# Linear attention and a rational feed-forward layer on one core: first unit in two halves of the head pairs, all of w_in cast by its DMA, early loads ordered by holds, a new list of steps

## Chip, cores and metric

The kernel runs on one core of one Trainium2 chip. The metric is the device time of the core in microseconds (us); smaller is better.

## The reference, cut

```python
# attention: batch 4, heads 8, sequence 768, head size 48
f = 1.0 / (1.0 + np.exp(-f_logit))
for t in range(S):
    state = f[:, :, t, :, None] * state + np.einsum('bhd,bhe->bhde', k[:, :, t], v[:, :, t])
    y[:, :, t] = np.einsum('bhd,bhde->bhe', q[:, :, t], state)
x = y.transpose(0, 2, 1, 3).reshape(B * S, H * D)        # 3072 x 384
# feed-forward: w_in 384 x 2048, w_out 2048 x 384
h = x @ w_in
P = a[0] + a[1] * h + a[2] * h**2 + a[3] * h**3
Q = 1.0 + np.abs(b[0]) * np.abs(h) + np.abs(b[1]) * h**2
out = (P / (Q + 1e-06)) @ w_out
```

## The kernel before

The work is cut into 12 units (3 chunks of 256 positions for each of 4 batch entries). One unit first goes through attention on all 8 heads: exp and log of f (`efl`), a running sum over positions by a triangular matmul (`cs`), exponentials of it (`A0`, `A1`), products with q and k (`mq`, `mk`), transposes (`T`) and their copy out of PSUM (`Te`), scores (`sc0`, `sc1`), masks (`m0`, `m1`), state (`sv`, `st`, `su`), `y`, and `xT` (`xe`). Then it goes through the feed-forward layer in two groups a and b of 8 column tiles: `h` with w_in, its bf16 copy `Y`, the polynomial on VectorE (`z q t s B P`), log and exp on ScalarE (`L E`), the product `g`, and the output product and its copy and store (`o O`). Group a needs w_in blocks 0 and 1, group b blocks 2 and 3. A hand-made list gives the order of all steps; each engine is given its own share of it in that order.

```python
STEPS = """
    cs:0 A1:0 mk:0 A0:0 mq:0 T:0 sv:0 al:0 Te:0 efl:1 sc0:0 m0:0 sc1:0 st:0 m1:0 y:0 cs:1 sw:0 xe:0
    ha1:0 su:0 A1:1 vl:3 A0:1 Ya1:0 mk:1 ha0:0 mq:1 T:1 hb0:0 Ya0:0 sv:1 Te:1 efl:2 za:0 qa:0 Ba:0 sc0:1
    Yb0:0 m0:1 hb1:0 Ua:0 al:1 sc1:1 Yb1:0 st:1 cs:2 sw:1 m1:1 zb:0 A1:2 ta:0 mk:2 y:1 su:1 qb:0 A0:2
    mq:2 sv:2 La0:0 xe:1 sa:0 tb:0 Ub:0 Bb:0 ha0:1 T:2 ha1:1 Ea:0 Pa:0 Ya0:1 Te:2 sc0:2 al:2 hb1:1 Lb0:0
    st:2 m0:2 Ya1:1 za:1 Yb1:1 hb0:1 sc1:2 ga:0 ta:1 qa:1 efl:3 Eb:0 cs:3 sb:0 m1:2 A1:3 Ua:1 mk:3 sw:2
    # ... 28 lines of the list cut ...
    oa0:9 Pb:10 oa1:9 Lb0:10 Yb1:11 Pa:11 Oa:9 qb:11 ob0:9 Eb:10 tb:11 zb:11 ob1:9 gb:10 Ub:11 La0:11
    Ob:9 oa0:10 Ea:11 Lb0:11 sb:11 oa1:10 Bb:11 Oa:10 Pb:11 ob0:10 ob1:10 Eb:11 Ob:10 ga:11 gb:11 oa0:11
    oa1:11 Oa:11 ob0:11 ob1:11 Ob:11
"""
P_BY_DMA = {4, 5, 6, 7, 9, 10, 11, 12, 13, 14, 15, 16, 17, 18, 19, 20, 21, 22}

U_BY_DMA = {2, 3, 4, 5, 6, 7, 8, 9, 11, 13, 15, 16, 17, 18, 19, 20, 21, 22}

TE_ON_ACT = {1, 2, 3, 4, 5, 8, 11}
O_ON_DVE = {(9, 0), (10, 0)}
# ... signature, constants and pools cut; every PSUM pool: psA 1 buffer, psr 2, ps1 1, pso 1 ...
    def load(n):
        c, u = units[n]
        at_[n] = dict(qk=qkp[n % NQK], ls=lsp[n % NQK], st=states[u], c=c, u=u)
        for name, src in (("fn", f_logit), ("kn", k), ("qn", q)):
            at_[n][name] = ld.tile([C, H, UB, D], F32, name=name)
            nc.sync.dma_start(out=at_[n][name].rearrange("p h b d -> p h (b d)"), in_=rows(src, n))

    def load_v(n):
        at_[n]["vn"] = vz[n % NV]
        for cc in range(UB):
            w = slice(CH * cc, CH * cc + CH)
            nc.gpsimd.dma_start(out=vz[n % NV][w, :, cc].rearrange("p h b d -> p h (b d)"), in_=rows(v, n)[w])
    # ... paired(), natural() cut ...
    def a_ef(n):
        s = at_[n]
        fl = "p h b d -> p (h b d)"
        ef = at.tile([C, H, UB, D], F32, name="ef")
        nc.scalar.activation(ef.rearrange(fl), s["fn"].rearrange(fl), AF.Exp, scale=-1.0)
        nc.scalar.activation(paired(s["ls"]), natural(ef), AF.Ln, bias=1.0)

    def a_cs(n):
        s = at_[n]
        cs = psr.tile([C, 2, 512], F32, name="cs", tag="r")
        for b in range(UB):
            for src in range(UB):
                nc.tensor.matmul(cs[:, b, 0:DM].rearrange("t (i p d) -> t i p d", i=2, p=HP),
                                 Us if src > b else U,
                                 s["ls"][:, :, src, :, 0:D].rearrange("t p i d -> t i p d"),
                                 start=(src == 0), stop=(src == UB - 1))
        s["cs"] = cs

    def a_exp(n, i):
        s = at_[n]
        t = at.tile([C, H, UB, D], F32, name=f"A{i}")
        nc.scalar.activation(t.rearrange("p h b d -> p b h d"),
                             s["cs"][:, :, 0:DM].rearrange("p b (h d) -> p b h d", h=H),
                             AF.Exp, scale=(-1.0, 1.0)[i])
        s["A", i] = t

    def a_mul(n, i):
        s = at_[n]
        nc.vector.tensor_mul(paired(s["qk"][:, i]), natural(s[("qn", "kn")[i]]), natural(s["A", i]))

    def a_T(n):
        s = at_[n]
        tp = psA.tile([P, UB, 2, HP, C], BF16, name="tp", tag="A")
        for b in range(UB):
            for i in range(2):
                for p in range(HP):
                    nc.tensor.transpose(tp[:, b, i, p, :],
                                        s["qk"][:, i, p, b].rearrange("t i d -> t (i d)"),
                                        ident)
        s["tp"] = tp
    # ... a_Te (copy of tp to qkT, by DVE or ACT), a_sv, a_sw cut ...
    def a_sc(n, half):
        s = at_[n]
        sc = psA.tile([C, 2, 2, UB, C], F32, name="sc", tag="A")
        for q_ in range(2):
            p = half * 2 + q_
            for b in range(UB):
                for i in range(2):
                    for cc in range(UB):
                        r, w = slice(64 * i, 64 * i + D), slice(CH * cc, CH * cc + CH)
                        nc.tensor.matmul(sc[w, i, q_, b, :], s["qkT"][r, b, 1, p, w], qcols(s, r, p, w),
                                         start=True, stop=True)
        s["sc", half] = sc
    def a_mask(n, half):
        s = at_[n]
        m = at.tile([C, 2, 2, UB, C], BF16, name=f"scm{half}")
        mb = bass.AP(tensor=mask.tensor, offset=mask.offset,
                     ap=[mask.ap[0], [0, 4], [1, UB * C]])
        nc.vector.tensor_mul(m.rearrange("s i q b t -> s (i q) (b t)"),
                             s["sc", half].rearrange("s i q b t -> s (i q) (b t)"), mb)
        s["scm", half] = m
    # ... a_y (many small matmuls: scm x v and q x state, into one psA tile), a_al, a_st cut ...
    def a_xe(n):
        s = at_[n]
        xTs[n] = xp.tile([P, KD, UB, C], BF16, name="xT")
        nc.scalar.activation(xTs[n], s["y"], AF.Copy, scale=sig[:, 0:1])
    # ... m_h to m_g cut: h = w_in x xT, y = bf16 copy of h (ACT), then z, h2, t, pb on DVE,
    #     lq and qi on ACT, gall = t * qi on DVE; two adds of each group may be done by a DMA ...
    def m_o(m, b, mms):

        if mms[0] == 0:
            if m < NUN - 2 or (m == NUN - 2 and b == 0):
                ops[m, b] = pso.tile([P, DM], F32, name="op")
            elif m == NUN - 2:
                ops[m, b] = ps1.tile([P, 512], F32, name="opl", tag="w1")[:, 0:DM]
            else:
                if b == 0:
                    ops["pair"] = psA.tile([P, 2, 512], F32, name="op2", tag="A")
                ops[m, b] = ops["pair"][:, b, 0:DM]
        for mm in mms:
            nc.tensor.matmul(ops[m, b], galls[m][:, mm, b * C:(b + 1) * C], w_out_sb[:, mm, :],
                             start=(mm == 0), stop=(mm == KF - 1))
    def load_w_in(g, dma_cast=True):
        cols = slice(g * WB * P, (g + 1) * WB * P)
        src = [moe_w_in[i * DM // 2:(i + 1) * DM // 2, cols].rearrange("(ko ki) n -> ki ko n", ki=P // 2)
               for i in range(2)]
        if dma_cast:
            for i in range(2):
                nc.gpsimd.dma_start(out=w_in_sb[i * P // 2:(i + 1) * P // 2, :, cols], in_=src[i])
        else:
            pool, tag = ((ms, "lq"), (gp, "gall"))[g]
            t = pool.tile([P, KD, WB * P], F32, name="wst", tag=tag, **(dict(bufs=1) if g == 0 else {}))
            nc.sync.dma_start(out=t[0:P // 2], in_=src[0])
            return (lambda: nc.scalar.dma_start(out=t[P // 2:P], in_=src[1]),
                    lambda: nc.gpsimd.tensor_copy(w_in_sb[:, :, cols], t))

    def load_w_out(g):
        nc.gpsimd.dma_start(out=w_out_sb[:, g * WB:(g + 1) * WB, :],
                            in_=moe_w_out[g * WB * P:(g + 1) * WB * P, :].rearrange("(ko ki) n -> ki ko n", ki=P))
    # ... loads of a and b cut ...
    load(0)
    casts = [load_w_in(0, False), load_w_in(1, False)]
    load(1)
    # ... U, Us, ident, mask, and on VectorE all memsets of zeros, vz, lsp, qkp; load_v(0) ...
    coefficients()
    busy(12)
    a_ef(0)
    for second, _ in casts:
        second()
    casts[0][1]()
    load_v(1)
    casts[1][1]()
    load_w_in(2)
    load_w_in(3)

    def after(n):

        src = (w_in_sb[0:1, 0, 3 * WB * P - 16:3 * WB * P], w_out_sb[0:1, 3 * WB - 1, 0:16])[n]
        nc.sync.dma_start(out=hold[0:1, n, :], in_=src)

    after(0)
    load(2)
    nc.gpsimd.tensor_copy(hold[0:1, 2, :], at_[2]["kn"][0:1, H - 1, UB - 1, 0:16])
    load_v(2)
    for g in range(KF // WB):
        load_w_out(g)
    after(1)
    # ... table of the steps cut ...
    warming, read = {"cs": 8, "T": 4, "sv": 3, "y": 4}, {0: 1}
    for token in STEPS.split():
        key, n = token.split(":")
        n = int(n)
        steps[key](n)
        if n == 0:
            busy(warming.get(key, 0))
        if key in ("efl", "mq", "mk"):
            read[n] = read.get(n, 0) + 1
            if read[n] == 3 and n + 3 < NUN:
                load(n + 3)
```

`busy(k)` issues k matmuls without use, meant to keep TensorE's granted clock up (a5 below has 14 more of them and a clock of 1.00 from 11.4 to 18.2 us, where the changed kernel had 0.51 in one run and 0.71 in another). A *hold* is a tiny copy or transfer of the last bytes of some load; what its engine issues afterwards starts only when that load has landed. In the profile of before SyncE waits 17.2 us for w_out: it issues nothing from 28.97 us until the hold goes at 46.26, and f of unit 3 follows at 46.88.

## Time and profile before

| | before |
|---|---|
| median of 3 runs (range) | 241.98 us (241.76 to 242.11) |
| span of the profiled run | 241.2 us |
| busy: PE / DVE / ACT | 87% / 88% / 85% |
| DVE's first feed-forward instruction (z) starts | 29.18 us |
| DVE's last instruction (gall) ends | 232.60 us |

The prediction below shows the slices, the start and the end. Two more views matter later. The first is the busy time of each engine by stretch; the columns are the stretch, its length, then busy us and number of instructions for PE, PEld, DVE, ACT and POOL, then the granted PE clock, DMA's load and GB/s:

```profile
0.00:30.00 30.00, 21.76 (x247) 13.50 (x250) 16.69 (x39) 11.59 (x14) 9.99 (x22) 0.89 1.08 192
30.00:40.00 10.00, 7.18 (x188) 5.65 (x187) 9.40 (x12) 9.02 (x11) 6.72 (x9) 0.94 0.80 115
40.00:60.00 20.00, 13.54 (x195) 10.10 (x194) 17.66 (x20) 16.77 (x17) 0.94 (x1) 0.84 1.21 220
```

DVE, the fuller engine, leaves 13.31 us free before 30 us, 0.60 us from 30 to 40 and 2.34 us from 40 to 60. The second view is SyncE's own queue, which shows the order of the transfers (start, us spent issuing, queue, line, operation, out<-in):

```profile
3.01 3.04 SPq L485 DMA_DIRECT2D wst<-in_moe_w_in_dram  x2
6.09 0.60 SPq L157 DMA_DIRECT2D fn<-in_f_logit_dram  x1
...
46.26 0.53 SPq L554 DMA_DIRECT2D hold<-w_out_sb  x1
```

The staged weights stand ahead of f of unit 1, and f of unit 3 may not be issued before 46.8 us, when the hold on w_out lets go.

### The profile page before, as it was taken

What the parts mean: (1) busy time and instruction counts of PE and PEld (TensorE: products, weight loads), DVE (VectorE), ACT (ScalarE), POOL (GpSimd) and SP (SyncE); (2) the same over time, 40 slices, a digit from 0 to 9 for tenths busy, and PEclk for the clock granted to TensorE, in tenths of its full rate; (3) what the DMA queues carried; (4) which work ended last, traced back from release to release, by engine and by line L of the source; (5) the groups of instructions that cost most, each with busy time, mean ns of one, the idle gap of its engine ahead of it and who ended that gap; (6) DMA issues with size and microseconds to landing.
All of it is one profiled execution on the core that took longest, in us unless ns stands there. A gap on an engine that the chain in (4) does not pass through costs nothing.

```text
span 241.2 us, 7061 instructions
## 1 busy us (share of the span) xinstructions
PE 209.4 (87%) x3091; PEld 150.6 (62%) x3095; DVE 212.3 (88%) x257; ACT 204.4 (85%) x200; POOL 63.7 (26%) x83
## 2 busy tenths in 40 slices
PE   4767968756989998998899999999999999997874
PEld 1245846535856787675666787766777777774442
DVE  6851599898989999999999999989999999999850
ACT  2404788969799999999799999999999999999940
POOL 5028046010403314233300522302513143223000
PEclk9995997987899999999999999999999999999999
DMA  5999959999999999999996699985969599999711
GB/s 136 213 210 195 211 96 150 170 254 255 242 242 231 190 227 236 221 226 231 203 216 141 124 211 252 199 108 120 144 122 196 114 176 207 207 191 209 171 65 65
DMA packets 62910, 44.49 MB, mean 184 GB/s; under 512 B 51616, under 2 KB 57504, under 8 KB 62880
## 3 DMA queue, kind: packets, MB, share of 16 engines
q0 software_dynamic: 20800, 23.60, 60.9%
q1 hardware_dynamic: 41376, 19.66, 33.2%
q10 hardware_dynamic: 704, 0.79, 1.7%
q8 instruction: 24, 0.39, 0.6%
q14 instruction: 6, 0.05, 0.1%
HBM read 25.17 MB, written 4.72 MB: 124 GB/s over the span
## 4 chain that ended last, share of the span: by engine, by line
DVE 42%; ACT 18%; PE 12%; issue 12%; DMA 12%; POOL 2%; POOLq 0%; DVEq 0%; ACTq 0%
DVE h L380 6%; DMA t<-pb 6%; DVE t L426 6%; DVE gall L446 5%; DVE scm L280 5%; ACT y L375 5%; DMA z<-h 4%; PE hp L361 4%; ACT lq L411 4%; DVE qkp L204 4%; DVE pb L429 3%; ACT qi L416 3%; DVE t L421 3%; DVE z L385 3%; PE op L463 3%
## 5 line engine op out<-in xcount | busy, mean ns | idle before, releaser
L361 PE MATMUL hp<-xT,w_in_sb 128*128 128x256 bf16 x576 | 71.7, 279 | 1.6 <-ACT y L375 1.2
L463 PE MATMUL op<-w_out_sb,gall 128*128 128x384 bf16 x368 | 65.3, 326 | 4.3 <-ACT osb L218 1.7
L361 PEld LDWEIGHTS <-w_in_sb 128*128 128x128 bf16 x576 | 56.0, 100 | 11.9 <-issue 2.6
L463 PEld LDWEIGHTS <-gall 128*128 128x128 bf16 x384 | 36.7, 98 | 28.1 <-issue 4.4
L375 ACT CAST y<-hp 128x1024 bf16<-128x1024 f32 x48 | 48.5, 1026 | 3.3 <-PE hp L361 2.8
L416 ACT ACTIVATE qi<-lq 128x2048 bf16<-128x2048 f32 x24 | 46.3, 1931 | 0.1
L411 ACT ACTIVATE lq<-z,sig 128x2048 f32<-128x2048 bf16 x22 | 44.5, 2024 | 2.1 <-DMA z<-h 2.0
L403 POOL DMA_DIRECT2D z<-h x18 | 17.3, 958 | 74.8 <-ACT ef L180 21.6
L435 POOL DMA_DIRECT2D t<-pb x18 | 18.7, 1037 | 60.2 <-DVE t L426 54.0
L280 DVE TENSOR_TENSOR scm<-sc,mask 128x1024 bf16<-128x1024 f32 x24 | 29.3, 1219 | 2.4 <-PE sc L264 2.3
L446 DVE TENSOR_TENSOR gall<-t,qi 128x2048 bf16<-128x2048 bf16 x24 | 29.0, 1217 | 0.6 <-DMA t<-pb 0.6
L380 DVE TENSOR_TENSOR h<-y 128x2048 bf16<-128x2048 bf16 x24 | 29.2, 1216 | 0.1
L426 DVE TENSOR_TENSOR t<-t,h 128x2048 bf16<-128x2048 bf16 x24 | 29.1, 1215 | 0.0
L197 ACT ACTIVATE A<-cs 128x768 f32<-128x768 f32 x24 | 18.7, 823 | 4.1 <-PE cs L188 4.0
L429 DVE TENSOR_SCALAR pb<-y,a_sb 128x2048 bf16<-128x2048 bf16 x24 | 19.6, 816 | 1.6 <-DMA t<-pb 1.6
L163 POOL DMA_DIRECT2D vz<-in_v_dram x24 | 20.1, 920 | 2.0 <-DVE vz L514 1.9
L421 DVE TENSOR_SCALAR t<-y,a_sb 128x2048 bf16<-128x2048 bf16 x24 | 19.5, 818 | 0.5 <-ACT y L375 0.5
L180 ACT ACTIVATE ef<-fn 128x768 f32<-128x768 f32 x12 | 10.4, 863 | 10.6 <-DMA fn<-in_f_logit_dram 10.6
L385 DVE TENSOR_SCALAR z<-y 128x2048 uint16<-128x2048 uint16 x24 | 16.5, 686 | 2.7 <-ACT y L375 2.6
L188 PE MATMUL cs<-lsp,U 128*128 128x384 bf16 x36 | 10.9, 359 | 8.6 <-ACT lsp L181 7.4
L315 PE MATMUL y<-scm,vz 128*32 128x128 bf16 (+1 forms) x768 | 15.6, 233 | 0.0
L212 PE MATMUL tp<-ident,qkp 128*128 128x128 bf16 x192 | 13.1, 223 | 2.7 <-DVE qkp L204 1.7
(72 smaller groups left out, 244.0 us busy)
## 6 DMA issues: line engine op xcount, KB each, us to landing
z<-h POOLq DMA_DIRECT2D x18, 512.0 KB, 5.9
t<-pb POOLq DMA_DIRECT2D x18, 512.0 KB, 6.6
fn<-in_f_logit_dram SPq DMA_DIRECT2D x12, 384.0 KB, 6.1
kn<-in_k_dram SPq DMA_DIRECT2D x12, 384.0 KB, 6.6
qn<-in_q_dram SPq DMA_DIRECT2D x12, 384.0 KB, 8.8
out_dram<-osb SPq DMA_DIRECT2D x24, 192.0 KB, 3.8
vz<-in_v_dram POOLq DMA_DIRECT2D x24, 96.0 KB, 6.9
w_out_sb<-in_moe_w_out_dram POOLq DMA_DIRECT2D x4, 384.0 KB, 8.7
```

What stands on the lines that cost most here:

```text
L280: nc.vector.tensor_mul(m.rearrange("s i q b t -> s (i q) (b t)"), s["sc", half].rearrange("s i q b t -> s (i q) (b t)"), mb)
L361: nc.tensor.matmul(hp[:, e, :], w_in_sb[:, kk, f * P:(f + 1) * P], xT[:, kk, :], start=(kk == 0), stop=(kk == KD - 1))
L375: nc.scalar.copy(part_of(tile_of(n, "y"), half), mg[n]["hp", half].rearrange("p a n -> p (a n)"))
L380: nc.vector.tensor_mul(s["h2"], s["y"], s["y"])
L385: nc.vector.tensor_scalar(s["z"].bitcast(U16), s["y"].bitcast(U16), 0x7FFF, None, op0=ALU.bitwise_and)
L411: nc.scalar.activation(lq if whole else part_of(lq, half), s["u"] if whole else s["u", half].rearrange("p a n -> p (a n)"), AF.Ln, scale=s ...
L416: nc.scalar.activation(part_of(tile_of(n, "qi"), part, parts), part_of(mg[n]["lq"], part, parts), AF.Exp, scale=-1.0)
L421: nc.vector.tensor_scalar(tile_of(n, "t", bufs=3), mg[n]["y"], a_sb[:, 3:4], a_sb[:, 2:3], op0=ALU.mult, op1=ALU.add)
L426: nc.vector.tensor_mul(s["t"], s["t"], s["h2"])
L429: nc.vector.tensor_scalar(tile_of(n, "pb"), mg[n]["y"], a_sb[:, 1:2], a_sb[:, 0:1], op0=ALU.mult, op1=ALU.add)
L446: nc.vector.tensor_mul(galls[m][:, lo:lo + w, :].rearrange("p a n -> p (a n)"), part_of(s["t"], part, parts), part_of(s["qi"], part, parts))
L463: nc.tensor.matmul(ops[m, b], galls[m][:, mm, b * C:(b + 1) * C], w_out_sb[:, mm, :], start=(mm == 0), stop=(mm == KF - 1))
```

## The change

The intent is to start VectorE's feed-forward stream earlier. Unit 0 is taken through attention in two halves of its head pairs, so that the engines overlap inside it; unit 1 is loaded ahead of the weights; w_in is converted by the transfer and no longer staged and cast by GpSimd; holds put the early transfers into one order. The list of steps is a new one from end to end, and a few copies and additions change engine.

```diff
--- before
+++ after
@@ the steps: unit 0 in two halves ("-" is the first), unit 1 interleaved; end of the list @@
-    cs:0 A1:0 mk:0 A0:0 mq:0 T:0 sv:0 al:0 Te:0 efl:1 sc0:0 m0:0 sc1:0 st:0 m1:0 y:0 cs:1 sw:0 xe:0
-    ha1:0 su:0 A1:1 vl:3 A0:1 Ya1:0 mk:1 ha0:0 mq:1 T:1 hb0:0 Ya0:0 sv:1 Te:1 efl:2 za:0 qa:0 Ba:0 sc0:1
+    efl-:0 efl:0 cs-:0 A0-:0 A1-:0 cs:0 A1:0 mk-:0 A0:0 mq-:0 T-:0 mk:0 mq:0 Te-:0 T:0 sc0:0 sv:0 Te:0
+    efl:1 m0:0 al:0 sc1:0 st:0 cs:1 A0:1 m1:0 y-:0 mq:1 y:0 A1:1 mk:1 sw:0 su:0 xe:0 T:1 Te:1 ha0:0
+    Ya0:0 ha1:0 sc0:1 sv:1 m0:1 Ya1:0 vl:3 al:1 st:1 sc1:1 za:0 efl:2 qa:0 cs:2 A1:2 ta:0 Ua:0 m1:1 sa:0
+    hb0:0 sw:1 Ba:0 y:1 mk:2 A0:2 hb1:0 La0:0 Pa:0 Yb0:0 Ea:0 su:1 xe:1 mq:2 Yb1:0 T:2 ga:0 ha1:1 Te:2
     # ... the other lines of the list are a new order too; cut ...
-    oa1:11 Oa:11 ob0:11 ob1:11 Ob:11
+    ob0:10 oa0:10 sb:11 Bb:11 ob1:10 Eb:11 ga:11 oa1:10 Oa:10 oa0:11 Pb:11 ob0:11 gb:11 ob1:11 oa1:11
+    Oa:11 Ob:10 Ob:11
@@ which adds a DMA does, and who makes which copy (choices per group or unit) @@
-U_BY_DMA = {2, 3, 4, 5, 6, 7, 8, 9, 11, 13, 15, 16, 17, 18, 19, 20, 21, 22}
-TE_ON_ACT = {1, 2, 3, 4, 5, 8, 11}
-O_ON_DVE = {(9, 0), (10, 0)}
+U_BY_DMA = {2, 3, 5, 6, 7, 8, 9, 11, 13, 14, 16, 17, 18, 19, 20, 21, 22, 23}
+TE_ON_ACT = {1, 2, 4, 5, 6, 11}
+O_ON_DVE = {(0, 1), (11, 1), (10, 1), (2, 0), (9, 1)}
     # ... P_BY_DMA: 8 in, 22 out ...
@@ load(n): unit 0 in 12 pieces of two heads @@
+            if n > 0:
+                nc.sync.dma_start(...whole tile...)
+        if n == 0:
+            for ps in HALVES:
+                for name, src in (("fn", f_logit), ("kn", k), ("qn", q)):
+                    for i in range(2):
+                        hs = slice(HP * i + ps.start, HP * i + ps.stop)
+                        nc.sync.dma_start(out=at_[n][name][:, hs].rearrange("t h b d -> t h (b d)"),
+                                          in_=rows(src, n)[:, hs])
# ... a_ef, a_cs, a_exp, a_mul, a_T, a_Te and a_y take a range ps of head pairs; cut ...
@@ a_sc @@
-        sc = psA.tile([C, 2, 2, UB, C], F32, name="sc", tag="A")
+        pool, tag = (psr, "r") if (n, half) == (0, 1) else (psA, "A")
+        sc = pool.tile([C, 2, 2, UB, C], F32, name="sc", tag=tag)
@@ load_w_in: no staging any more, each block two DMAs that cast, from GpSimd @@
@@ before the steps @@
     load(0)
-    casts = [load_w_in(0, False), load_w_in(1, False)]
-    load(1)
+    nc.gpsimd.memset(vz[0].rearrange("p h c b d -> p (h c b d)").bitcast(F32), 0.0)
+    load_v(0)
     # ... half of the memsets go from VectorE to GpSimd; coefficients() goes behind step m1:0 ...
-    a_ef(0)
-    for second, _ in casts:
-        second()
-    casts[0][1]()
+    load(1)
+    hold_back(nc.gpsimd, last_of(1, "kn"), 0)
+    for g in range(2):
+        load_w_in(g)
     load_v(1)
-    casts[1][1]()
-    load_w_in(2)
-    load_w_in(3)
-    after(0)                       # SyncE waits for w_in block 2
+    hold_back(nc.sync, w_in_end(0), 1)
     load(2)
-    nc.gpsimd.tensor_copy(hold[0:1, 2, :], at_[2]["kn"][0:1, H - 1, UB - 1, 0:16])
+    hold_back(nc.gpsimd, last_of(2, "fn"), 2)
+    for g in range(2, KF // WB):
+        load_w_in(g)
     load_v(2)
     for g in range(KF // WB):
         load_w_out(g)
-    after(1)
+    hold_back(nc.sync, w_out_sb[0:1, 3 * WB - 1, 0:16], 3)
@@ in the loop over the steps @@
-    warming, read = {"cs": 8, "T": 4, "sv": 3, "y": 4}, {0: 1}
+    warming, read = {"cs": 3, "T": 1, "sc1": 2, "y-": 1, "y": 3}, {}
+        if n == 0 and key[:-1] in halves and key[-1] == "-":
+            halves[key[:-1]](n, HALVES[0])
+        elif n == 0 and key in halves:
+            halves[key](n, HALVES[1])
+        else:
+            steps[key](n)
```

## The prediction

> **What bounds the kernel now.** I read the 40 slices first, because a busy share over the whole span mixes stages:
>
> ```profile
> PE   4767968756989998998899999999999999997874
> DVE  6851599898989999999999999989999999999850
> ACT  2404788969799999999799999999999999999940
> PEclk9995997987899999999999999999999999999999
> DMA  5999959999999999999996699985969599999711
> ```
>
> A slice is 6.03 us. From slice 5 (30 us) to slice 37, VectorE (DVE) stands at 8 or 9, and ScalarE (ACT) from slice 11 at 9 but for one; neither has room. Only the first five slices (DVE 6 8 5 1 5, and much of those digits is memsets) and the last two are slack. Busy time by stretch confirms it: from 60 to 220 us DVE is busy 156.6 of 160 us. So the end is set by when DVE's stream of work starts, how much work is in it, and what follows its last instruction.
>
> Then I read the timeline of the start, for what delays that stream:
>
> ```profile
> 5.54 0.84 ACT L180 ACTIVATE ef<-fn 128x768 f32<-128x768 f32 x1 [3.52 <-DMA fn<-in_f_logit_dram]
> 9.06 1.51 ACT L197 ACTIVATE A<-cs 128x768 f32<-128x768 f32 x2 [1.80 <-PE cs L188]
> 10.53 0.95 DVE L204 TENSOR_TENSOR qkp<-kn,A 128x768 bf16<-128x768 f32 x1
> 13.51 1.23 DVE L218 COPY qkT<-tp 128x2048 bf16<-128x2048 bf16 x1 [1.16 <-PE tp L212]
> 16.13 1.23 DVE L280 TENSOR_TENSOR scm<-sc,mask 128x1024 bf16<-128x1024 f32 x1 [1.40 <-PE sc L264]
> 17.41 0.42 PE L264 MATMUL sc<-qkT 48*64 48x128 bf16 x16 [1.33 <-DVE scm L280]
> 21.99 0.90 ACT L348 ACTIVATE xT<-y,sig 128x768 bf16<-128x768 f32 x1 [0.96 <-PE y L315]
> 29.18 0.69 DVE L385 TENSOR_SCALAR z<-y 128x2048 uint16<-128x2048 uint16 x1 [1.45 <-ACT y L375]
> ```
>
> This is one chain through unit 0, each engine waiting for the previous one. The second sc product waits for the first mask (1.33 us), since both use the one psA buffer. The MoE stream of DVE begins with z at 29.18.
>
> The end, in the timelines of DVE, PE and ACT:
>
> ```profile
> 230.25 2.35 DVE L446 TENSOR_TENSOR gall<-t,qi 128x2048 bf16<-128x2048 bf16 x2
> 231.53 2.77 PE L463 MATMUL op<-w_out_sb,gall 128*128 128x384 bf16 x16 [0.74 <-DVE gall L446]
> 234.87 2.76 PE L463 MATMUL op<-w_out_sb,gall 128*128 128x384 bf16 x16 [0.57 <-ACT osb L218]
> 237.67 0.48 ACT L218 COPY osb<-op 128x384 f32<-128x384 f32 x1 [2.85 <-PE op L463]
> ```
>
> After DVE's last instruction (232.60), 8.6 us of output products, a copy and a store remain.
>
> [...] the DMA row is 9 in slices 1 to 3 although three engines issue. So reordering can choose who comes first, but cannot make the first 20 us carry more. [...] by stretch the clock is 0.50 from 19 to 25 us, after a thin stretch at 15 to 19.
>
> **The change part by part.**
>
> *Halves of unit 0.* The loads become 12 DMAs of two heads each. SyncE now needs about 0.5 us per issue (0.45 to 1.10 for the whole ones), so the first half of fn is issued by 1.7 us and I expect it at 4.5, but the second half of fn, seventh and eighth in line, is issued at 4.4 and lands near 7.5. The instruction order shows that ACT does both halves of exp/log before the first A[...]. The gain comes after that. The pieces then overlap:[...] transposes of half 1 under products of half 2; first half of qkT 11.8 to 12.5[...]; sc at 12.6; second qkT to 13.2; mask 13.2 to 14.4 (before: 16.13); the second sc is in psr, so its mask need not wait: with the state (0.3) in between, 14.7 to 15.9 (before: 19.1). Half of y runs under that mask, the other half after it takes about 1.3 at half clock: xT near 17.3 instead of 21.99. DVE is ready in time, since 3.5 us of memsets (0.70+0.48+0.91+2x0.70) go to GpSimd or off the path; the 1.6 us of coefficients now stand after the second mask and their first half (0.8) is hidden by y.
>
> *Unit 1 ahead of the weights.* load(1) now comes before w_in. Before, fn of unit 1 landed at 19.3; now about 12 (1.8 MB at the speed of the before trace, whose rates of 114 to 308 GB/s add up to that by 10.5 us, plus landing). So cs, A, products and transposes of unit 1 run by 20.5 instead of 29.
>
> *w_in cast by its DMA.* Two GpSimd casts (1.46 and 1.50 us) and their staging go. Bytes read are the same. GpSimd issues it only after kn of unit 1 has landed (about 13.5) plus a 0.9 us copy; a block is two issues of 0.63, and before, block 2 was issued at 20.5 to 21.8 and released its follower at 25.35, 4.2 us after its last issue. So block 0 at 15.7 + 4.2 = 20, block 1 near 22.5. The first h can go at 20.5 (before 24.98, both blocks by 20.5), the second y cast ends near 25, and z starts at **25.0 instead of 29.2**. The first mask of unit 1 (1.2 us) is already done then; before it came later. DVE's stream is 4.2 + 1.2 = 5.4 us ahead.
>
> *What takes some back.* Unit 2 waits for w_in block 0 (load issued 20.6, fn near 26.5), and w_in blocks 2 and 3 wait for fn of unit 2: GpSimd issues block 2 at 27.4, landing about 33, block 3 about 35.5. [...]y of unit 1 stands behind the first h that needs block 2. I added up DVE's work in program order with measured start-to-start times: between z at 25.0 and the first instruction that needs block 3 stand 11 us, so DVE gets there at 36 and may wait until 38 or 39: minus 2 to 3 us in the bad case.
>
> *The later weights.* fn of unit 3 still waits for three blocks of w_out, which follow w_in in GpSimd's queue; I expect it at 50 (before 50.99). That wait exists already:
>
> ```profile
> 50.99 0.84 ACT L180 ACTIVATE ef<-fn 128x768 f32<-128x768 f32 x1 [2.02 <-DMA fn<-in_f_logit_dram]
> ```
>
> But the new order puts more ACT work (31.8 against 27.0 us) and 4.9 us more DVE work ahead of it, which is just what an earlier start needs.
>
> *Steady work.* DVE: one more qkT (+1.14), three more osb copies (+1.6), two U additions fewer (-2.3), halves +0.3: about +0.7. ACT: three osb and one qkT fewer[...]: -0.9 by the same sum. PE: two more U groups, 16 matmuls of 512 columns, about 3.5 us, on an engine that is 87% busy. No gain here.
>
> *Tail.* Both output blocks of the last unit now do their first half of the contraction before the last gall, so after it come 2 x 8 matmuls (2.77 us), a copy (0.5) and a store (3.05): 6.5 us instead of 8.6, -2.1. But the last U is now a DMA (z<-h took 4.7 to 6.2 us near the end, plus 0.86 issue), then log 2.0 and exp 1.9 and the product: near 11 us, where DVE has 8.8 us between that z and the last gall. Up to 2 us come back. I count -1.2.
>
> Sum: -5.4 at the start, +0.8 for the wait at blocks 2 and 3 (2 to 3 us in about one case of three), +0.7 DVE work, -1.2 tail, and some -1 for the wait at unit 3 that no longer binds: 241.98 - 6.1 = **235.9 us**.
>
> **Rivals.** (a) *The transfers set the start anyway.* For it: DMA is saturated from 4 to 27 us, so block 1 of w_in cannot land much before 22; if GpSimd's hold leaves the engines idle, 24. Then the gain at the start is 2 to 3 us and the total 238 to 239. Against it: before, both blocks were cast by 20.6, 1.4 us ahead of the xT that needs them, while fn of unit 1 came late (19.3): the chain and not the weights set the start. (b) *Blocks 2 and 3 or fn of unit 3 become the new wait*: DVE idles from 36 to 40 or near 50, and all but 2 us are given back: 238 to 240. For it: before, they landed before need. (c) *No new wait binds and the tail gain is whole*: 241.98 - 5.4 - 1 - 2.1 = 233.5. (d) *A mid-stream stall*: the new order of the DMA additions costs some us; the DVE of before idles only 3.4 us in 60 to 220, so there is little to win and some to lose: +1 to +2.
>
> **Range and chances.** 2% faster is under 237.1. The middle is 1.2 us below that; (a) or (b) in full would miss it, and I give them together about 30%. A slower kernel needs new stalls of more than 10 us. Range 232.5 to 239.5.
>
> **What would show it.** Right: xT of unit 0 starts at 16.5 to 18.5, the first z at 24 to 26, DVE idle in 30 to 60 us no more than 5 us, the span behind DVE's last gall 6.3 to 7. Wrong: the first h waits for w_in beyond 22; DVE waits of over 3 us for y casts at 33 to 40; ACT's wait for fn of unit 3 over 4 us; DVE's idle time in 60 to 220 over 5 us. If xT is early but z starts near 28, rival (a) holds.

## The result

A ratio here is the mean time of one kernel's runs over the mean of the other's in the same rounds, so it is not quite the ratio of the medians. Executions over 1.5% slower than the fastest of the same kernel are left out of the means. All outputs are right.

| | before | after |
|---|---|---|
| median, 4 runs each (range) | 241.87 us (241.42 to 242.11) | 233.8 us (233.4 to 235.25) |
| ratio, 95% interval | | 0.9679 (0.9635 to 0.9724): faster |
| span of the profiled run | 241.2 us | 231.3 us |
| busy PE / DVE / ACT | 87 / 88 / 85% | 91 / 92 / 87% |
| exp of the second half (whole) of f starts | 5.54 us | 8.45 us |
| xT of unit 0 starts | 21.99 us | 20.72 us |
| first z starts | 29.18 us | 27.15 us |
| DVE's last gall ends, and span behind it | 232.60, 8.60 us | 223.63, 7.67 us |

The profiled run of before took 243.2 us, 1.3 us above its median, so the two traces differ by 9.9 us where the medians differ by 8.1.

The 40 slices of after:

```profile
DVE  5686599999999999999999999999999999999950
ACT  4424889997999999999999999999998999799950
PEclk9959979999979999999999999999999999999998
DMA  7999999999999999999999999876599969998502
```

From the sixth slice (a slice is now 5.78 us) DVE stands at 9 without a break until the last two, where before it fell to 8 in five. The PE clock row has a 5 in the third slice, in the middle of the new start.

The timeline of ScalarE (start, us, engine, line, operation, out<-in, shapes, count, and in brackets how long it had been idle and for whom):

```profile
8.45 0.52 ACT L203 ACTIVATE ef<-fn 128x384 f32<-128x384 f32 x1 [3.02 <-DMA fn<-in_f_logit_dram]
9.43 1.62 ACT L226 ACTIVATE A<-cs 128x384 f32<-128x384 f32 x4
20.72 0.90 ACT L387 ACTIVATE xT<-y,sig 128x768 bf16<-128x768 f32 x1 [0.96 <-PE y L352]
47.35 0.86 ACT L201 ACTIVATE ef<-fn 128x768 f32<-128x768 f32 x1
```

The second half of f is waited for until 8.45 us, and A starts at 9.43, later than in the kernel before (9.06). xT comes 1.3 us earlier than before and not 4.7. The exp of unit 3, in the last line, has no wait in brackets any more.

The timelines of PE and VectorE at the start:

```profile
9.57 0.24 PE L217 MATMUL cs<-lsp,U 128*128 128x192 bf16 x1 [3.61 <-ACT lsp L204]
```

```profile
25.74 1.23 DVE L315 TENSOR_TENSOR scm<-sc,mask 128x1024 bf16<-128x1024 f32 x1 [3.85 <-PE sc L299]
27.15 0.70 DVE L424 TENSOR_SCALAR z<-y 128x2048 uint16<-128x2048 uint16 x1
```

PE (TensorE) stood for 3.61 us waiting for that second half; the stretch table gives a granted clock of 0.51 from 11.4 to 18.2 us. On VectorE a mask of unit 1 and a state product (1.23 + 0.35 us) are now done ahead of z.

SyncE's queue, and the stretches that answer to those of before:

```profile
17.29 0.62 SPq L573 DMA_DIRECT2D hold<-w_in_sb  x1
...
39.39 0.50 SPq L573 DMA_DIRECT2D hold<-w_out_sb  x1
```

```profile
0.00:30.00 30.00, 22.77 (x294) 13.92 (x295) 19.54 (x41) 14.78 (x22) 16.84 (x36) 0.86 1.07 180
30.00:40.00 10.00, 8.28 (x147) 6.79 (x145) 10.00 (x12) 9.53 (x9) 2.88 (x5) 0.92 1.41 198
40.00:60.00 20.00, 18.54 (x265) 13.66 (x263) 20.00 (x24) 18.66 (x20) 5.44 (x6) 1.00 1.11 237
```

w_in block 0 has landed by 17.3 us, and the hold on w_out lets go 6.9 us earlier than before. The first 20 us carry no more than before (169 GB/s against 193); what changed is who comes first: the exp of unit 1's f runs at 11.39 us and not at 19.31. From 30 to 60 us DVE is busy without a gap: the 2.94 us of waits there are gone.

The end, in the timelines of VectorE, PE and ScalarE:

```profile
222.40 1.23 DVE L485 TENSOR_TENSOR gall<-t,qi 128x2048 bf16<-128x2048 bf16 x1 [1.04 <-ACT qi L455]
```

```profile
223.68 2.77 PE L502 MATMUL op<-w_out_sb,gall 128*128 128x384 bf16 x16 [0.63 <-DVE gall L485]
```

```profile
226.49 0.48 ACT L249 COPY osb<-op 128x384 f32<-128x384 f32 x1 [3.76 <-PE op L502]
```

Only 16 output matmuls and not two runs of 16 follow the last gall. But VectorE's block, whose last matmul is the eighth, is copied only at 227.00 us, behind ScalarE's copy of the other block (2.91 us of waiting), with which it shares a PSUM tile; the span ends at 231.3.

Where the 9.9 us between the traces are, all from the two DVE timelines:

| term | predicted | after | the same kernel again (control, below) |
|---|---|---|---|
| DVE's stream ahead when z starts (z, plus mask and state of unit 1 done earlier) | -5.4 | -2.0 - 1.6 = -3.6 | -3.4 - 1.6 = -5.0 |
| DVE's waits between 30 us and the last gall (before 6.95 us) | +0.8 - 1.0 = -0.2 | 2.05: -4.9 | 4.00: -2.95 |
| DVE's work between (what is left over) | +0.7 | -0.5 | -0.25 |
| span behind the last gall | -1.2 | -0.9 | -0.9 |
| sum | -6.1 | -9.9 | -9.1 |

A sum that came out near the truth was made of terms that did not. The experiments ask why.

### The profile page after: what moved, and what is told of

Same layout as the page of the kernel before. It is cut to its first block, busy times and chain, and to the rows that moved or that the text cites.

```text
span 231.3 us, 7110 instructions
## 1 busy us (share of the span) xinstructions
PE 211.0 (91%) x3106; PEld 150.1 (65%) x3106; DVE 212.1 (92%) x257; ACT 202.1 (87%) x202; POOL 66.3 (29%) x91
## 4 chain that ended last, share of the span: by engine, by line
DVE 58%; PE 21%; issue 10%; DMA 6%; ACT 3%; SPq 1%; POOL 0%; DVEq 0%; POOLq 0%; ACTq 0%
DVE scm L315 8%; DVE h L419 8%; DVE gall L485 8%; DVE t L465 7%; PE op L502 7%; PE hp L400 6%; DVE t L460 5%; DVE qkp L232 5%; DVE pb L468 5%; DVE z L424 4%; DVE qkT L249 2%; PE y L352 2%; DMA z<-h 2%; DVE t L476 2%; DVE state L381 2%
## 5 line engine op out<-in xcount | busy, mean ns | idle before, releaser
L400 PE MATMUL hp<-xT,w_in_sb 128*128 128x256 bf16 x576 | 70.2, 275 | 0.6 <-ACT y L414 0.2
L400 PEld LDWEIGHTS <-w_in_sb 128*128 128x128 bf16 x576 | 55.1, 99 | 11.1 <-issue 2.0
L502 PEld LDWEIGHTS <-gall 128*128 128x128 bf16 x384 | 36.1, 98 | 26.4 <-issue 2.2
L450 ACT ACTIVATE lq<-z,sig 128x2048 f32<-128x2048 bf16 x20 | 40.4, 2020 | 2.9 <-DMA z<-h 2.8
L474 POOL DMA_DIRECT2D t<-pb x18 | 17.5, 975 | 45.7 <-DVE t L465 30.1
L226 ACT ACTIVATE A<-cs 128x768 f32<-128x768 f32 (+1 forms) x26 | 18.7, 767 | 4.2 <-PE cs L217 4.1
L174 POOL DMA_DIRECT2D vz<-in_v_dram x24 | 21.8, 1131 | 0.3 <-POOL vz L531 0.3
L217 PE MATMUL cs<-lsp,U 128*128 128x384 bf16 (+1 forms) x39 | 10.9, 341 | 6.2 <-ACT lsp L204 6.1
L243 PE MATMUL tp<-ident,qkp 128*128 128x128 bf16 x192 | 13.8, 227 | 2.6 <-DVE qkp L232 2.4
L243 PEld LDWEIGHTS <-qkp 128*128 128x128 bf16 x192 | 12.2, 101 | 5.5 <-DVE qkp L232 3.5
```

What stands on the lines that cost most here:

```text
L243: nc.tensor.transpose(tp[:, b, i, p, :], s["qk"][:, i, ps.start + p, b].rearrange("t i d -> t (i d)"), ident)
L400: nc.tensor.matmul(hp[:, e, :], w_in_sb[:, kk, f * P:(f + 1) * P], xT[:, kk, :], start=(kk == 0), stop=(kk == KD - 1))
L450: nc.scalar.activation(lq if whole else part_of(lq, half), s["u"] if whole else s["u", half].rearrange("p a n -> p (a n)"), AF.Ln, scale=s ...
```

## The experiments

**Theory.** The gain is that of the new transfer order and the new step order together. The halves themselves bring little: the start is set by when transfers land (the second half of f, then w_in block 2 near 30 us), so an earlier xT is given back. **Rivals.** (i) The halves shorten the chain and that is the gain. (ii) The transfer order alone brings the gain. (iii) TensorE's half clock between 11 and 18 us holds the start. (iv) The output blocks' shared PSUM tile costs the missing part of the tail.

Four calls; the kernels of one call ran on one chip and share its runs of the kernel before. Calls 1 and 2 were on the same chip, 3 and 4 on two others. Times are medians.

| call | kernel | us (range) | ratio to before, 95% interval |
|---|---|---|---|
| 1 | before | 242.76 (242.13 to 243.28) | |
| 1 | a1_whole: unit 0 whole | 233.09 (232.2 to 233.96) | 0.9607 (0.9575 to 0.9639) |
| 1 | a2_old_loads: old transfers | 239.1 (238.23 to 240.02) | 0.9855 (0.9821 to 0.989) |
| 1 | a3_new_loads: new transfers alone | 243.01 (242.81 to 243.45) | 1.0018 (0.9999 to 1.0038) |
| 1 | a4_f_first: both halves of f first | 232.93 (232.05 to 234.23) | 0.9618 (0.9585 to 0.9652) |
| 2 | before | 243.17 (241.14 to 244.45) | |
| 2 | c0_control: the changed kernel | 234.25 (233.03 to 234.93) | 0.9614 (0.9559 to 0.9669) |
| 2 | a1b_whole: a1 again | 232.69 (232.48 to 232.94) | 0.9553 (0.9509 to 0.9596) |
| 2 | a5_pe_warm: PE kept busy | 235.37 (234.38 to 235.71) | 0.9656 (0.9609 to 0.9702) |
| 2 | a8_f_first_hold_f | 231.96 (230.81 to 233.81) | 0.953 (0.9451 to 0.9608) |
| 3 | before | 242.82 (240.85 to 245.37) | |
| 3 | a7_own_psum: output blocks apart | 233.66 (233.17 to 234.6) | 0.9638 (0.9603 to 0.9673) |
| 3 | a9_no_second_hold | 235.47 (234.94 to 235.89) | 0.9705 (0.9668 to 0.9742) |
| 3 | a10_whole_hold_f | 232.74 (232.16 to 233.97) | 0.9604 (0.9567 to 0.9642) |
| 4 | before | 243.49 (240.95 to 245.42) | |
| 4 | a11_best | 231.07 (230.44 to 232.58) | 0.9493 (0.9438 to 0.9549) |

### Undo the halves

```diff
-    efl-:0 efl:0 cs-:0 A0-:0 A1-:0 cs:0 A1:0 mk-:0 A0:0 mq-:0 T-:0 mk:0 mq:0 Te-:0 T:0 sc0:0 sv:0 Te:0
-    efl:1 m0:0 al:0 sc1:0 st:0 cs:1 A0:1 m1:0 y-:0 mq:1 y:0 ...
+    efl:0 cs:0 A1:0 mk:0 A0:0 mq:0 T:0 Te:0 sc0:0 sv:0
+    efl:1 m0:0 al:0 sc1:0 st:0 cs:1 A0:1 m1:0 mq:1 y:0 ...
# and load(0) as the other units: three whole DMAs
```

> The changed kernel with unit 0 loaded and computed whole again (loads, exp/log, cumulative sums, products, transposes, y); new loads, holds, split of work and order of steps stay. Theory H (the halves shorten the start, and that is most of the gain): xT of unit 0 starts at 22.5 us or later instead of 20.72, the first z about 2 us later than 27.15, time 236 to 238 us. Theory L (load order and the waits at 30 to 80 us that it removes are most of the gain): xT within 1 us of 20.72, since the whole fn lands before the second half does, time 233 to 235.

Measured: 233.09 us. A starts at 8.29 us, xT at 20.21, z at 26.64, all earlier than in the profile of after. From ScalarE's timeline:

```profile
5.68 0.84 ACT L155 ACTIVATE ef<-fn 128x768 f32<-128x768 f32 x1 [3.67 <-DMA fn<-in_f_logit_dram]
20.21 0.90 ACT L341 ACTIVATE xT<-y,sig 128x768 bf16<-128x768 f32 x1 [0.30 <-PE y L306]
```

The second call repeated it beside the changed kernel itself.

> Unit 0 whole once more (the same kernel as a1_whole), now beside the changed kernel on one chip. If the halves bring nothing as the change makes them (second half of f lands at 8.45 us, later than the whole f did): within 0.5% of the control either way. If the halves were worth 1% or more, this is slower than the control by over 2 us, and the 0.9607 of the first call was the chip.

> The changed kernel itself, so that the others of this call have it on the same chip: 0.965 to 0.970 of before (233 to 235 us), xT near 20.7, first z near 27.2.

Measured: a1b 232.69 us (232.48 to 232.94), the control 234.25 us (233.03 to 234.93). The kernel without halves is 1.6 us (0.6%) *faster* on the same chip; its interval of the ratio to before just overlaps the control's, but its slowest run is faster than the control's fastest. So the halves as made bring nothing, and rival (i) falls. About half a us of the difference lies at the other end: behind the last gall the kernels with unit 0 whole (a1, a1b and a10 below) take 7.16 to 7.23 us, after and the control 7.67 and 7.66; the cause was not looked for.

The control itself came out a little faster against before than had been expected (0.965 to 0.970), with xT and z 1.4 us earlier than in the profile of after.

Why the halves do not shorten the start is seen in the queue: in after, the 12 issues for unit 0 take SyncE from 0.74 to 6.87 us at about half a us for each piece of 96 KB, while the first two issues of 384 KB in before took no longer (0.45 and 0.57 us), and the second half of f is the seventh and eighth of them; the exp of the whole f starts at 5.68 (a1), that of the second half at 8.45.

### Undo the transfers

```diff
     load(0)
+    casts = [load_w_in(0, False), load_w_in(1, False)]   # staged, as before
+    load(1)
...                                                      # new order of loads and holds taken out
+        if token == "efl:0":
+            # second halves of the staging, the two GpSimd casts, load_v(1), load_w_in(2), load_w_in(3),
+            # hold on w_in block 2, load(2), hold on kn of unit 2, load_v(2), w_out, hold: as before
```

> The changed kernel with the transfers of before: two blocks of w_in staged as f32 ahead of unit 1 and cast by GpSimd, no hold on k of unit 1, unit 2 held until block 2 of w_in, w_out held until k of unit 2. Halves and order of steps stay. Theory L: unit 1's f lands near 19 us again, it stands before xT on ACT, xT at 22 or later, first z near 29, and f of unit 3 near 50 us stalls DVE by more than 4 us in 30 to 60: time 239 to 242. Theory H: 235 to 237.

Measured: 239.1 us, 6.0 us slower than a1 and 6.2 slower than a4 of the same call. The new order of steps wants unit 1 early and does not get it. ScalarE's timeline:

```profile
20.76 0.84 ACT L201 ACTIVATE ef<-fn 128x768 f32<-128x768 f32 x1 [8.59 <-DMA fn<-in_f_logit_dram]
```

ScalarE waits 8.59 us for f of unit 1 (in after it runs at 11.39 us after a wait of 0.34), y of unit 0 and all that follows stands behind the sums of unit 1 on PE, and xT comes at 27.89. The loss is not all due to the order of the transfers: unit 0 is still loaded in 12 pieces here, so the staged weights are issued from 7.21 us and not from 3.01, the first GpSimd cast runs at 19.35 and not at 16.37, and f of unit 1 comes 1.5 us later than in before (20.76 against 19.31). The new steps with the transfers of before at their own times were not run. VectorE's idle time came at 30 to 40 us (3.13 us); the stall at unit 3 that was expected did not come (none from 40 to 60).

### Only the new transfers

```diff
# the kernel before's STEPS, sets and warming; unit 0 whole; from the change: load order, holds,
# w_in cast by DMA, memsets shared with GpSimd, coefficients behind m1:0
```

> The kernel before with only the new loads, holds, w_in cast by DMA, memsets shared with GpSimd and later coefficients; unit 0 whole, order of steps, warming and split of work of before. Theory L: f of unit 3 lands at 44 to 46 instead of 50, DVE idle in 30 to 80 falls from 4.1 us to under 1.5, time 236 to 238. Theory S (the new order of steps fills the waits; loads alone only move them): DVE idle in 30 to 80 stays over 3 us and time 239.5 to 242.

Measured: 243.01 us, ratio 1.0018: nothing, and slower than both expected ranges. xT comes at 20.34 us and z at 26.94, much as in after (20.72 and 27.15), so an early z alone does not do it, and rival (ii) falls. The stretch from 30 to 40 us and PE's timeline show where it was given back:

```profile
30.00:40.00 10.00, 8.93 (x167) 6.64 (x171) 5.32 (x7) 4.74 (x7) 3.45 (x5) 0.71 1.37 197
```

```profile
30.36 2.72 PE L354 MATMUL hp<-xT,w_in_sb 128*128 128x256 bf16 x12 [3.60 <-ACT lsp L158]
```

DVE is busy for only 5.32 of 10 us. The old order puts `hb0:0`, the first use of w_in block 2, directly behind `T:1`; PE stands at it for 3.60 us, and the scores and masks of unit 1 stand behind it. The profile names a log of ScalarE as what ended that wait. These matmuls do not read it, while GpSimd had issued w_in from 24.69 to 27.17 us, and such a block took 3.7 to 6.3 us to land in this run, so I take the weights to be the cause; that is inferred from the times, not shown. In a1b, where block 2 was issued at the same time (24.66 us), the profile does name the weights, at nearly the same time:

```profile
30.44 2.72 PE L354 MATMUL hp<-xT,w_in_sb 128*128 128x256 bf16 x12 [1.95 <-DMA w_in_sb<-in_moe_w_in_dram]
```

The new list puts `hb0:0` behind the scores and the state of unit 1 and the sums of unit 2, so that PE and VectorE have these to do in the meantime. A later stall (2.87 us of DVE idle between 80 and 140 us) takes more back; its cause is open. Loads and steps were made for one another: either alone brings little or nothing.

### An earlier chain: f first, or PE kept busy

```diff
-            for ps in HALVES:
-                for name, src in (("fn", f_logit), ("kn", k), ("qn", q)):
+                for name, src, ps in (("fn", f_logit, HALVES[0]), ("fn", f_logit, HALVES[1]),
+                                      ("kn", k, HALVES[0]), ("qn", q, HALVES[0]),
+                                      ("kn", k, HALVES[1]), ("qn", q, HALVES[1])):
```

> The changed kernel with both halves of f of unit 0 issued first, then k and q of half 0, then of half 1 (same 12 DMAs). The second exp of unit 0 waits until 8.45 us for f now. If the second half of f is what delays the first A (9.43), A starts at 7.0 to 8.0, xT 1 to 2 us earlier, time 231.5 to 233. If the path to xT is set elsewhere (PE at half clock and its order), xT moves less than 0.7 us and the time stays at 233.3 to 234.3.

```diff
-    warming, read = {"cs": 3, "T": 1, "sc1": 2, "y-": 1, "y": 3}, {}
+    warming, read = {"cs-": 14, "cs": 3, "T": 1, "sc1": 2, "y-": 1, "y": 3}, {}
```

> The changed kernel with 14 more warming matmuls after the first half's cumulative sum, where PE idles for 3.6 us now and then runs at a granted clock of 0.51 from 11.4 to 18.2 us. If the half clock is what makes the chain miss the predicted 17.3: clock near 1.0 from 11 to 18, xT at 19.0 to 19.7 instead of 20.72, first z 1 to 1.5 us earlier, and the time 0.5 to 1.5 us lower unless w_in's third block stops it. If the chain is set by DVE alone: xT moves under 0.4 us.

Both did to the start what they were made for. In a4 the second half's exp runs at 6.25 us, the clock is 1.00 from 5 to 17, xT comes at 16.48 us and z at 24.05: the prediction's figures for these (17.3 and 25.0) and better. In a5 the clock is 1.00 from 6 to 18 us, xT comes at 18.24 (control 19.36). The times did not follow: a4 took 232.93 us against 233.09 for a1 of the same call, whose xT is 3.7 us later; a5 took 235.37 against 234.25 for the control, with intervals that overlap. (a4's time lies in the range that was expected of a gain, 231.5 to 233, but that range was set against the first run of the change. The changed kernel was not in a4's call; against before the two have the same ratio, 0.9618 and 0.9614.) PE's timeline of the control, a4 and a5 shows one and the same wait:

```profile
30.14 2.08 PE L400 MATMUL hp<-xT,w_in_sb 128*128 128x256 bf16 x9 [2.33 <-DMA w_in_sb<-in_moe_w_in_dram]
```

```profile
30.10 2.29 PE L402 MATMUL hp<-xT,w_in_sb 128*128 128x256 bf16 x10 [3.73 <-DMA w_in_sb<-in_moe_w_in_dram]
```

```profile
29.72 2.51 PE L400 MATMUL hp<-xT,w_in_sb 128*128 128x256 bf16 x11 [2.90 <-DMA w_in_sb<-in_moe_w_in_dram]
```

The first h of group b starts at 29.7 to 30.1 us in all three, however early the chain is. That wait takes part of what the chain gains: a4 leads the control by 1.7 us at the first z (24.05 against 25.79) and by 0.7 at the second (37.54 against 38.23), a5 by 1.0 and 0.9. The profile of after fits: its xT is 1.4 us later than the control's, it has no wait there (the matmuls go at 29.87 us), and its span is no longer (231.3 against 232.1). So the half clock is real, but a1, which has it too (0.50 from 14 to 18 us), is as fast as a4, which has not, and rival (iii) finds no support. A gain of up to 1 us from the clock is not excluded, since a5 loses its lead elsewhere: there is 2.9 us of DVE idle between 80 and 140 us, around a PE pause of 1.92 us at 115.45 that the profile puts down to nothing; that stays open, and with it the 1.1 us by which a5 is slower.

### Weights earlier

The weights stand behind a hold for k of unit 1. The next edit lets them go as soon as f of unit 1 has landed, in the kernel with f first:

```diff
 # on top of a4_f_first
-    hold_back(nc.gpsimd, last_of(1, "kn"), 0)
+    hold_back(nc.gpsimd, last_of(1, "fn"), 0)
```

> Both halves of f first, as in a4_f_first, and w_in's first two blocks released by f of unit 1 instead of k of unit 1. In a4_f_first xT came 4.2 us earlier but the end only 1.4 us, since PE then waited 3.7 us at 30.1 for w_in block 2; DMA stood nearly idle from 13.2 to 15.5. If the transfers are the bound of the start now: that gap closes, w_in block 2 lands 1.5 to 2 us earlier, PE's wait shrinks to about 2 us, time 1 to 1.5 us under a4_f_first (0.955 to 0.958 of before). If not: as a4_f_first, 0.96 to 0.963.

Measured: 231.96 us, 2.3 us under the control of the same call; but its runs scatter (230.81 to 233.81), its interval overlaps the control's, and a1b of the same call, without halves and without earlier weights, is only 0.7 us slower (232.69, ratio 0.9553 against 0.953). A gain over the control is likely, one over a1b is not shown. GpSimd issues w_in at 11.32 us instead of 12.90 (control; 12.96 in a4), and PE's wait for block 2 moves with it:

```profile
28.56 2.72 PE L402 MATMUL hp<-xT,w_in_sb 128*128 128x256 bf16 x12 [1.63 <-DMA w_in_sb<-in_moe_w_in_dram]
```

The same hold without the halves:

> Unit 0 whole, with w_in released by f of unit 1: what the halves are worth once the transfers are ordered better. If the halves are only carried along, this is as fast as a8_f_first_hold_f (0.953 of before) within 0.4%. If halves with f first do shorten the way (xT at 16.5 to 17.8 there, 20 to 20.7 here), it is 1 to 2 us slower than a8 (0.957 to 0.961) and PE does not wait for w_in block 2 at all.

Measured: 232.74 us, ratio 0.9604, no better than a1 without it (0.9607 and 0.9553). Its w_in goes at 11.94 us, but xT is at 20.28 and z at 26.71, where a8 has 17.84 and 24.27. It was expected that PE would not wait for block 2 at all; it waits 1.49 us, until 30.23, hardly earlier than in a1b (30.44), since block 2 goes only at 23.84 here (22.75 in a8, 24.66 in a1b). So this run does not tell whether earlier weights pay only where the chain is early too; that is a guess. (a8 and a10 ran on different chips, each beside its own runs of the kernel before.)

All nine profiles in which PE waits for block 2 with the new list and the new transfers, put side by side, show what follows it. The block is waited for until 28.56 us in a8, 29.57 in a11 (below), 29.72 in a5, 30.10 to 30.44 in a4, the control, a10, a7 (below) and a1b, and 31.38 in a1; the second z of DVE, the first of group b, starts at 35.86, 36.87, 37.34, 37.54 to 38.39, and 39.05. In the middle five xT lies anywhere from 16.48 to 20.28 us and moves that z by no more than 0.9. From there to the end of the last gall it is 184.7 to 186.5 us in all but a5 (188.6).

Taking away the other hold, which lets f of unit 2 go ahead of blocks 2 and 3:

```diff
 # on top of a8_f_first_hold_f
-    hold_back(nc.gpsimd, last_of(2, "fn"), 2)
```

> a8_f_first_hold_f without the second hold of GpSimd's queue, so that blocks 2 and 3 of w_in are issued right behind blocks 0 and 1, beside unit 2's f, k and q. If the order of transfers is the bound of the start: block 2 lands by 26 to 27, PE no longer waits for w_in, f of unit 2 lands 1 to 3 us later than 22.5, time 230 to 231.5. If f of unit 2 is what counts as much: the second cumulative sum holds PE up instead, time as a8 or up to 1.5 us worse.

Measured: 235.47 us, ratio 0.9705 against 0.953 for a8 (another chip; the intervals are apart), worse than both cases expected. PE has no wait for w_in left, but ScalarE has this one:

```profile
27.96 0.84 ACT L203 ACTIVATE ef<-fn 128x768 f32<-128x768 f32 x1 [4.05 <-DMA fn<-in_f_logit_dram]
```

The wait changed places: f of unit 2 lands late, and DVE idles 4.12 us between 30 and 40 us, against 0.33 in a8 and 1.33 in the control. That is near the prediction's rivals (a) and (b), with an operand that neither names: in this stretch the hold chose which of the two loads was waited for, and letting the weights go first cost 1.7% against a8.

### The tail

```diff
-                if b == 0:
-                    ops["pair"] = psA.tile([P, 2, 512], F32, name="op2", tag="A")
-                ops[m, b] = ops["pair"][:, b, 0:DM]
+                pool, tag = ((psA, "A"), (psr, "r"))[b]
+                ops[m, b] = pool.tile([P, 2, 512], F32, name="op2", tag=tag)[:, 0, 0:DM]
```

> The changed kernel with the two output blocks of the last unit in PSUM tiles of their own instead of two halves of one. I predicted 6.5 us from the last gall to the end; it took 7.67, since the copy of the second block (DVE, 227.00) waits for the copy of the first (ACT, 226.49) and for all 16 matmuls. If the shared tile is the reason: DVE's copy starts about 1.4 us before ACT's, gall to end falls to 6.5 to 7.1 us, time 0.5 to 1.1 us less. If the stores set it: gall to end stays at 7.4 or more.

Measured: 233.66 us, and the span behind the last gall is 7.65 us (231.8 - 224.15), as in the control (7.66). VectorE's and ScalarE's timelines:

```profile
225.71 0.56 DVE L249 COPY osb<-op 128x384 f32<-128x384 f32 x1 [1.10 <-PE op L501]
```

```profile
227.01 0.48 ACT L249 COPY osb<-op 128x384 f32<-128x384 f32 x1 [3.76 <-PE op L501]
```

With tiles of their own VectorE copies its block at 225.71 us instead of 227.82 in the control, and ahead of ScalarE's copy instead of behind it, so the shared tile did serialize the two copies. The end does not move, and rival (iv) falls as it stood: SyncE issues the stores in the order of the list, `Oa:11 Ob:10 Ob:11`, so two finished blocks stand behind ScalarE's copy, and three stores then go out together: the profile has no DMA traffic from 226 to 228 us and 229 and 358 GB/s in the two us after. The last kernel therefore takes a8, the own tiles, and the stores in the order in which their copies are done:

```diff
 # on top of a8_f_first_hold_f and a7_own_psum, the end of the list
-    gb:11 ob1:11 oa1:11 Oa:11 Ob:10 Ob:11
+    gb:11 Ob:10 ob1:11 Ob:11 oa1:11 Oa:11
```

> Both findings together: f first and w_in released by f of unit 1 (a8_f_first_hold_f), and at the end tiles of their own with the stores issued in the order in which the copies can finish (second block of unit 10, second of unit 11, then the first of unit 11). In a7_own_psum the second copy came 2.1 us earlier (225.71 against 227.82) but the end stayed, since three stores stand in SyncE's queue behind the copy at 227.01. If that queue order sets the tail: last gall's end to the end of the span falls from 7.6 to 6.2 to 6.7 us and the time is 230 to 231.5 us, 0.945 to 0.950 of before. If the stores' own time sets it: 7.2 us or more, 0.953.

Measured: 231.07 us (230.44 to 232.58), ratio 0.9493; faster than before by 5.1%, and lower than any other version's ratio, though its interval overlaps those of a8 and a1b and it ran on a chip of its own. The end of ScalarE's timeline and VectorE's last gall:

```profile
221.43 1.23 DVE L449 TENSOR_TENSOR gall<-t,qi 128x2048 bf16<-128x2048 bf16 x1 [1.55 <-ACT qi L419]
```

```profile
225.52 0.48 ACT L213 COPY osb<-op 128x384 f32<-128x384 f32 x1 [3.76 <-PE op L465]
```

The span behind the last gall is 229.2 - 222.66 = 6.54 us, the figure that the prediction had expected of the change (6.5). Only one store is left behind the last copy. This gain of 1.1 us (7.65 to 6.54) is read from the traces; the times of a8 and a11 alone do not show it. The order of the stores without the own tiles was not run.

## Why the prediction was right or wrong

The predicted 235.9 us was 2.1 us above the median of 233.8, inside the range, and "faster" came true. The working is another matter: of its four signs of being right, the profile of after shows one (DVE idle from 30 to 60 us, none) and misses three (xT 20.72 us, z 27.15, span behind the last gall 7.67); none of its signs of being wrong came.

- **Start chain: wrong.** The step "the second half of fn ... lands near 7.5", and from it "xT near 17.3", failed. The half was there at 8.45 us and xT at 20.72 (19.36 in the control). It missed three things. The half second per issue counts for each of 12 pieces (seen, but the landing put too early); PE stands idle meanwhile and then runs at a clock of 0.51 (0.71 in the control); and the new list puts the sums of unit 1 and useless matmuls ahead of y on PE: they run from 15.96 to 18.05 us. The first half of y needs only the first mask, which ended at 15.64, and the text had it run under the second mask, which ended at 17.31; it starts at 18.05. The 4.7 us expected of xT were 1.3.
- **What the start is worth: right in part, for another reason.** The text made z and the work ahead of it 5.4 us early; 3.6 came in the profiled run, 5.0 in the control. w_in block 0 landed at 17.3 us and not at 20, so the weights were ready where the chain was not: k of unit 1 was there at 12.87 and not 13.5, the hold's copy took 0.19 us and not 0.9, and the text added 4.2 us to the end of the block's last issue, where the kernel before took 3.6 from that end (21.8 to 25.35). What the text had as a bad case, a wait for blocks 2 and 3, is the rule, though after itself had none: the control, a1, a1b, a4, a5, a8 and a10 have 1.5 to 3.7 us of PE wait for block 2, of which DVE lost 0.3 to 2.2 us between 30 and 40 us. a4 against a1 shows an early chain lose its lead: 2.6 us at the first z, 1.5 at the second behind that wait, 0.2 in the medians. Rival (a) had the right idea (transfers set the start) but the wrong block: block 2, not block 1.
- **Later waits: the term that was mis-sized most.** The text gave -0.2 us net for waits after the start; -4.9 came in the profiled run and -2.95 in the control. DVE's idle time from 40 to 220 us fell from 5.72 us (2.34 + 1.17 + 0.86 + 1.35) to 1.01. The text knew of the wait at unit 3, and said that it expects f of unit 3 "at 50 (before 50.99)". It came before 47.35 us, with the hold on w_out 6.9 us earlier, because w_out was issued from 28.1 us and not from 35.4: it stands behind a hold for unit 2, and unit 2 was loaded from 17.95 us (behind w_in block 0) and not from 25.98 (behind block 2). And the text said of the middle that there is "little to win and some to lose" (rival d), while a new list of steps for all 12 units was half of the change. Which part of the list is worth what was not separated.
- **Old loads or old steps: not foreseen.** The text summed parts as though each had its own gain. a2 and a3 show that they do not add: the new steps with the old transfers, as a2 has them, are worth about 1.5%, the new transfers with the old steps nothing, both together 3.2% (the first run) to 3.9% (the control).
- **Tail: size right, reason wrong.** -0.9 against -1.2. Of the 2.1 us that fewer matmuls should save the text gave part back to the chain of the last group. ScalarE's last exponential did hold up the last gall by 1.04 us (1.77 in the control), but the 6.5 us behind the gall were missed by 1.2 us through the shared tile and the order of the stores, which the text did not look at; a11, with both changed, gets them. (The text's own terms, 2.77, 0.5 and 3.05 us, add to 6.3.)
- **Steady work: off by about 1 us.** Predicted +0.7 us on DVE, left over -0.5 and -0.25; this is a remainder, and where the 1 us lies was not traced. The pieces of unit 0 took, in the profile of after: the half products 0.55 to 0.56 us (0.95 whole in before), so that four took 2.2 us where two whole ones took 1.9, which is the +0.3 that the text estimated for the halves; the half copies of qkT 0.69 (1.23 whole), the half exp and log 0.52 (0.84 whole). For PE the text gave 3.5 us to 16 matmuls of 512 columns; in before two pairs of them start 0.44 us apart (132.34 and 132.78), which makes 3.5 of 16.

So the total was good because a start that was counted too high and a middle that was counted too low cancelled; that is luck. Open are the PE pause of 1.9 us in a5, the idle time after 80 us in a3, and why the same kernel's xT came at 20.72 us in one run and 19.36 in another (with granted clocks of 0.51 and 0.71 at that place; no cause was tested).

## What to carry to other kernels

When a start is bound by transfers, draw the queue of issues first: an issue of a quarter of the bytes took no less time here (about 0.5 us), so pieces delay whatever is seventh in line (the second half of f: 8.45 us, where the whole f of a1 came at 5.68), and the first thing to ask of each piece is whether the very next instruction can use it. Order of transfers and order of steps are one design; test them together, and look for the next operand to land (here w_in block 2) before counting an earlier chain as a gain. At the end of a kernel, order the stores by when their copies are done, since a store that waits in its queue held up those behind it here (span behind the last gall 7.65 us in a7, 6.54 in a11).

## Further measurements

- One issue is short against its transfer (about 0.5 us, against a median of 3.6 to 3.7 us from issue to landing), but many in a row are not: 12 issues of 96 KB took SyncE 6.1 us (0.74 to 6.87), and the second half of f came at 8.45 us where the whole one came at 5.68 (a1). An issue of 96 KB took as long as one of 384 KB (0.45 and 0.57 us for the first two of before; later ones took up to 6.97).
- With the same instructions on VectorE and GpSimd, VectorE's second pair of mask casts took one of two durations, beside GpSimd's memsets from 5.1 to 7.9 us (the casts start at 4.99 us, the memsets at 5.09 and 5.10); why was not shown. The first line below is from VectorE's timeline of after, the second from that of the control, the same kernel:

```profile
4.99 2.97 DVE L548 CAST mask<-U 64x64 f32<-64x64 bf16 x2
```

```profile
4.99 0.73 DVE L548 CAST mask<-U 64x64 f32<-64x64 bf16 x2
```

  Of the 13 profiles with these memsets on GpSimd, seven have the long form (2.97 us, ending when the memsets end) and six the short one; with the short form GpSimd's first two memsets are the longer ones (0.57 and 1.07 us instead of 0.53 and 0.96). In after VectorE was waiting for ScalarE until 10.3 us anyway, so it cost nothing; in a8 and a11, whose chain is earlier, VectorE's first product starts at 8.1 us straight behind these casts.
- After a PE pause of 3.61 us the granted clock was 0.51, and with a filler in that pause (a5) it was 1.00; the end came no earlier (235.37 against 234.25 us).
- From the end of the last copy to the end of the span it took 3.05 us (before) and 3.20 us (a11) where one store of 192 KB was left, and 4.31 us (a7) where three went out together.
